# A first product turned round: tokens stationary, 512 weight columns moving

## The chip, the cores and the metric
One NeuronCore of a Trainium2 chip runs the whole program. The metric is device time in microseconds. TensorE multiplies, VectorE and ScalarE do elementwise work and bring results out of PSUM, GpSimd (POOL) does some elementwise work in SBUF, and SyncE (SP) issues the DMAs.

## The reference
Three stages follow one another. `r, k, v, w` have the shape (4, 8, 768, 48); `x` becomes 3072 tokens of 384 values.
```
# attention, per batch and head, over t:
y[t] = r[t] @ (state + (u*k[t]) outer v[t]);  state = w[t]*state + k[t] outer v[t]
# feed-forward, w_in is float64 in memory:
h = x @ w_in            # 3072 x 2048
g = h * cos(h);  x2 = g @ w_out        # 3072 x 384
# soft mixture of experts, 8 experts of 4 slots:
logits = x2 @ phi;  d = softmax over tokens;  slot_input = d.T @ x2
slot_out[e] = relu(slot_input[e] @ w1[e]) @ w2[e]
out = softmax over slots(logits) @ slot_out
```

## The kernel before
The tokens are cut into 24 blocks of 128 (index j) for attention and into 12 groups of 256 (index g) for the feed-forward part. The weights come as float64 and are decoded to float32 by integer steps (raw, abs, mx, d1, d2a, d2b); w_in is then kept as two rounded parts, hi and lo, in four tiles `wu` of 512 columns (whi, wn, wc). x is kept as two parts too (xh, xl), so that one product of the pair needs three matmuls per 128 of the 384 contracted rows: hi by hi, hi by lo, lo by hi.

The first product is b_h (L448 to L464): for a tile (g, i), i from 0 to 7, and each half mm it takes 128 columns of w_in as the stationary block and moves 256 tokens, 9 matmuls a half. A tile is 128 features by 512 (two halves of 256 tokens) in one PSUM bank. Four elementwise steps make g = h cos h of it: turns (ScalarE, L474), rest (VectorE, L478), cos (ScalarE, L482), mul (VectorE, L486). The logits are formed without the second product: p_sb holds w_out @ phi, and l (b_l, L507) multiplies g by it. gT (L494) transposes g on TensorE to tokens by features, gc (L499) copies it from PSUM to SBUF as `gt`, and E (s_e_pe, L603) sums the tokens of `gt` with the softmax weights dt. Between l and E of a group lie sum, lc, max, exp, xt, xr, xd, dT and dc: the logits gathered, the running maximum, the exponentials, and their transpose. es adds a group's E to the running sum. After the last group come si (the sum times w_out, L778), the experts (L797, L837) and the output (L868, L870).

Every step's place is written out by hand in the list HEAD: one string with names such as `h.3.1`, and each engine runs its instructions in the order of the list, SP its DMAs too. Buffers: g has 4, gt 12, the PSUM pools for h, gT, l 2, 1 and 1, and ps_a, shared by attention and late tiles, 3. A step that takes a new buffer waits for the last reader of the old one. "close" gives the decoding buffers back, "att" those of attention and issues the first six loads of expert weights; "we" issues five more, which take the place of wu tiles and of x.

Of the kernel before, what the change touches and what calls it, by code (L numbers as in the profile page):

```python
# [21 lines left out]
def rwkv_moe_kernel(ctx: ExitStack, tc: tile.TileContext, r, k, v, w, u, w_in, w_out, phi, w1, w2, cst, out):  # L22
# [7 lines left out]
    C = 64  # L30
# [6 lines left out]
    NBK = MF // 2  # L37
# [16 lines left out]
    g_p = b_stack.enter_context(tc.tile_pool(name="g", bufs=4, side="right"))  # L54
    gt_p = b_stack.enter_context(tc.tile_pool(name="gt", bufs=12, side="right"))
# [50 lines left out]
    vn_t, rz_t, l_t, ks_t, ksn_t, q_t, bv_t, z_t = ({} for _ in range(8))  # L106
# [243 lines left out]
    def e_abs(x, n, hf=None):  # L350
        if not hf:
# [94 lines left out]
    LAST = (NG - 1, NBK - 1)  # L446

    def b_h(g, i, mm):  # L448
        if mm == 0:
            pool, tag = (ps_a, "a") if NBK * g + i >= ATT else (ps_h, "h")  # L450
            hp = pool.tile([128, 2, G], F32, tag=tag, name=f"h{g}_{i}")
            h_t[g, i] = [hp[:, 0], hp[:, 1], hp]
        elif (g, i) == LAST:
            h_t[g, i][1] = ps_t.tile([128, 2, G], F32, tag="t", name=f"h{g}_{i}b")[:, 0]
        hp = h_t[g, i][mm]
        xh, xl = xh_t[g], xl_t[g]
        m = 2 * i + mm
# [12 lines left out]
    def b_turns(g, i, mm=None):  # L470
        if not mm:
            g_t[g, i] = g_p.tile([128, 2, G], F32, tag="g", name=f"g{g}_{i}")
        gt, hp = bank(g, i, mm)
        nc.scalar.activation(gt.bitcast(I32), hp, AF.Copy, bias=0.25, scale=1.0 / TWO_PI)  # L474

    def b_rest(g, i, mm=None):
        gt, hp = bank(g, i, mm)
        nc.vector.scalar_tensor_tensor(out=gt, in0=gt.bitcast(I32), scalar=-TWO_PI, in1=hp, op0=ALU.mult, op1=ALU.add)  # L478

    def b_cos(g, i, mm=None):  # L480
        gt, _ = bank(g, i, mm)
# [35 lines left out]
    def s_logits(g):  # L517
# [62 lines left out]
    def s_dc(g):  # L582
# [4 lines left out]
        sm[g] = (dt_, *sm[g][0:2])  # L587
# [58 lines left out]
    if True:  # L646
# [54 lines left out]
        step = {"tab": exp_table, "quart": lambda g: s_quarters(g, sm[g][0]), "esl": lambda g, hf: s_e(g, slice(hf * 256, hf * 256 + 256)),  # L701
# [57 lines left out]
        with tc.manual_schedule(engines=ORDERED):  # L759
# [155 lines left out]
raw.o.0 abs.o.1 mx.o.1 U.1 st.1.0 lr.3 d1.o.1 y.0 z.1.1 wf.2 yb.0 xh.0 lz.1 rz.1.0 d2a.o.1 xl.0 whi.0 wn.0.0 st.1.1 wc.0.0 lk.2
kT.2 scan.2 wn.0.1 abs.o.0 rz.1.1 d2b.o.1 mx.o.0 abs.o.2 ks.2 d1.o.0 mx.o.2 d2a.o.0 y.1 bv.1 yb.1 oT.3 oc.3 sr.2 d1.o.2 lr.2
wc.0.1 xh.1 raw.i.1 z.2.0 d2b.o.0 abs.i.1 kN.2 xl.1 oT.2 oT.1 ksn.2 oc.2 oc.1 d2a.o.2 oT.0 oc.0 mx.i.1 lw.4 h.0.2.0 d2b.o.2 oT.5
rT.2 lv.2 d1.i.1 d2a.i.1 raw.i.4 abs.i.4 h.0.2.1 oc.5 sp.2 d2b.i.1 oT.4 oc.4 lw.3 lk.3 lz.2 wT.3 whi.1 wf.3 om.0 L.2 mx.i.4 d1.i.4
# [150 lines left out]
```

## Time and profile before

| | before |
|---|---|
| runs | 542.59, 543.63, 544.12 us |
| median of the runs | 543.63 us |
| span of the profiled execution | 542.5 us |
| TensorE busy | 502.9 us, 93% |
| VectorE busy | 435.2 us, 80% |
| ScalarE busy | 310.7 us, 57% |
| granted TensorE clock, mean | 0.980 |

The span runs from the first to the last instruction of the profiled execution; its own time is that span and the little around it, and it stands 1.1 us below the median of the runs. A matmul's busy time is its latency, some 0.28 us, and matmuls overlap; the pace is read from start to start.

### The profile page before, as it was taken

Reading aid. Unit: us, or ns where it says so; the run is one execution under the profiler, and the core shown is the slowest. Engines: PE = TensorE matmul, PEld = TensorE weight load, DVE = VectorE, ACT = ScalarE, POOL = GpSimd, SP = SyncE. Lnnn points to the kernel's source line nnn. Section 1 sums busy time; section 2 is a strip of 40 time slices with the busy share of each in tenths; the row PEclk is TensorE's granted clock in tenths of the full one; section 3 lists DMA queues with packets and bytes.
Section 4 is the critical chain, followed back from the end, with each engine's and each line's share of the span. In section 5 each row is a group of like instructions: output and inputs, shape, how many; then the busy total and the mean of one; then the engine's idle time right before and its main releaser. Section 6 shows DMA issues by size and latency. Waiting matters only on the chain.

```text
span 542.5 us, 16245 instructions
## 1 busy us (share of the span) xinstructions
PE 502.9 (93%) x6850; PEld 436.4 (80%) x6850; DVE 435.2 (80%) x826; ACT 310.7 (57%) x655; POOL 125.4 (23%) x163
## 2 busy tenths in 40 slices
PE   2769879989999999999999999999999999998994
PEld 1547668879898898999988989989998989894673
DVE  4999998998889879887879788989878877666423
ACT  3356567646747555676555665755657646666421
POOL 4520120254044213221420331352033100000400
PEclk9977998999999999999999999999999999999998
DMA  9994656444332432421440442065031565188958
GB/s 218 258 238 105 176 115 183 125 76 75 74 59 46 76 59 50 79 37 30 76 74 1 75 89 45 17 111 83 16 61 31 229 252 220 29 322 311 403 181 272
DMA packets 146713, 67.52 MB, mean 124 GB/s; under 512 B 127569, under 2 KB 134737, under 8 KB 146641
## 3 DMA queue, kind: packets, MB, share of 16 engines
q1 hardware_dynamic: 146640, 66.49, 48.4%
q8 instruction: 54, 0.88, 0.7%
q14 instruction: 19, 0.15, 0.1%
HBM read 61.75 MB, written 4.72 MB: 123 GB/s over the span
## 4 chain that ended last, share of the span: by engine, by line
PE 67%; DVE 18%; ACT 5%; DMA 4%; issue 2%; SPq 2%; DVEq 0%; ACTq 0%
PE h L462 10%; PE h L464 10%; PE h L463 10%; PE gT L494 6%; PE l L507 4%; PE E L603 3%; PE A L208 3%; PE y L288 3%; PE U L259 2%; DMA vz<-in_v_dram 2%; PE hps L797 2%; DMA rawi<-in_moe_w_in_dram 2%; PE so L837 2%; DVE L L222 2%; DVE pt L164 2%
## 5 line engine op out<-in xcount | busy, mean ns | idle before, releaser
L462 PE MATMUL h<-x,wu 128*128 128x256 f32 x573 | 171.5, 299 | 1.4 <-DVE g L486 1.3
L464 PE MATMUL h<-x,wu 128*128 128x256 f32 x573 | 160.9, 281 | 0.0
L463 PE MATMUL h<-x,wu 128*128 128x256 f32 x573 | 160.8, 281 | 0.0
L462 PEld LDWEIGHTS h<-x,wu 128*128 128x128 f32 x573 | 108.7, 190 | 3.6 <-DVE g L486 1.7
L463 PEld LDWEIGHTS h<-x,wu 128*128 128x128 f32 x573 | 108.8, 190 | 0.2
L464 PEld LDWEIGHTS h<-x,wu 128*128 128x128 f32 x573 | 108.5, 189 | 0.0
L482 ACT ACTIVATE g<-g,half_pi 128x512 f32<-128x512 f32 (+1 forms) x97 | 69.4, 719 | 44.7 <-DVE g L478 43.7
L486 DVE TENSOR_TENSOR g<-g,h 128x512 f32<-128x512 f32 x96 | 64.8, 677 | 26.7 <-ACT g L482 26.1
L474 ACT ACTIVATE g<-h 128x512 int32<-128x512 f32 x96 | 57.1, 596 | 42.0 <-PE h L464 32.6
L478 DVE SCALAR_TENSOR_TENSOR g<-g,h 128x512 f32<-128x512 int32 x96 | 65.0, 678 | 14.9 <-ACT g L474 13.9
L251 POOL TENSOR_TENSOR bv<-vz,bo 64x384 f32<-64x384 f32 x48 | 43.8, 914 | 139.5 <-DVE bo L243 54.6
L499 ACT COPY gt<-gT 128x512 f32<-128x512 f32 x89 | 51.6, 584 | 28.7 <-PE gT L494 28.1
L494 PE MATMUL gT<-cs,g 128*128 128x128 f32 x384 | 58.1, 275 | 0.3 <-ACT gt L499 0.2
L494 PEld LDWEIGHTS gT<-cs,g 128*128 128x128 f32 x384 | 43.7, 140 | 6.0 <-issue 3.7
L169 POOL TENSOR_TENSOR ru<-rn,u_b 128x384 f32<-128x384 f32 x24 | 27.5, 1145 | 57.2 <-issue 19.5
L193 POOL MEMSET L<- 64x512 f32 x32 | 16.6, 520 | 96.0 <-PE y L288 81.5
L156 DVE TENSOR_TENSOR_SCAN qt<-wf,one_b 128x520 f32<-128x520 f32 x24 | 30.6, 1275 | 7.3 <-ACT wf L151 7.3
L222 DVE TENSOR_TENSOR L<-A,cs 64x512 f32<-64x512 f32 x48 | 33.0, 688 | 4.0 <-PE A L208 2.9
L274 ACT COPY rzs<-z 64x192 f32<-64x192 f32 x96 | 33.4, 348 | 3.6 <-DVE z L269 2.6
L187 DVE TENSOR_TENSOR L<-rT,pt 64x512 f32<-64x512 f32 x48 | 32.9, 686 | 1.6 <-PE rT L141 0.6
L164 DVE TENSOR_TENSOR_SCAN pt<-wf,ini_f 128x520 f32<-128x520 f32 x24 | 31.7, 1320 | 0.1
L208 PE MATMUL A<-L,ks 128*64 128x64 f32 (+1 forms) x768 | 27.7, 223 | 3.2 <-DVE ks L199 2.1
(172 smaller groups left out, 837.8 us busy)
## 6 DMA issues: line engine op xcount, KB each, us to landing
we<-in_moe_w_dram SPq DMA_DIRECT2D x16, 1536.0 KB, 10.4
rawi<-in_moe_w_in_dram SPq DMA_DIRECT2D x7, 768.0 KB, 5.5
wn<-in_w_dram SPq DMA_DIRECT2D x24, 192.0 KB, 4.0
kn<-in_k_dram SPq DMA_DIRECT2D x24, 192.0 KB, 4.0
rn<-in_r_dram SPq DMA_DIRECT2D x24, 192.0 KB, 3.8
vz<-in_v_dram SPq DMA_DIRECT2D x48, 96.0 KB, 3.1
rzs<-in_v_dram SPq DMA_DIRECT2D x96, 48.0 KB, 2.8
out_dram<-ob SPq DMA_DIRECT2D x17, 256.0 KB, 3.6
```

Source lines behind the costliest of these rows:

```text
L208: nc.tensor.matmul(ps[64 - 64 * a:128 - 64 * a, s, :], lhsT=ks[k, s, :], rhs=L[k, a, s, :], start=True, stop=True)
L222: nc.vector.tensor_tensor(out=L[h, a], in0=ps[h], in1=mask[h].unsqueeze(1).to_broadcast([64, NS, C]), op=ALU.mult)
L251: nc.gpsimd.tensor_tensor(out=bv[h], in0=vn_t[j][h, :, c, :], in1=bo[h].to_broadcast([64, H, D]), op=ALU.mult)
L462: nc.tensor.matmul(hp, lhsT=wh, rhs=xh[:, c, :], start=(c == 0), stop=False)
L463: nc.tensor.matmul(hp, lhsT=wh, rhs=xl[:, c, :], start=False, stop=False)
L464: nc.tensor.matmul(hp, lhsT=wl, rhs=xh[:, c, :], start=False, stop=(c == KD - 1))
L474: nc.scalar.activation(gt.bitcast(I32), hp, AF.Copy, bias=0.25, scale=1.0 / TWO_PI)
L478: nc.vector.scalar_tensor_tensor(out=gt, in0=gt.bitcast(I32), scalar=-TWO_PI, in1=hp, op0=ALU.mult, op1=ALU.add)
L482: nc.scalar.activation(gt, gt, AF.Sin, bias=half_pi[:, 0:1])
L486: nc.vector.tensor_tensor(out=gt, in0=gt, in1=hp, op=ALU.mult)
L494: nc.tensor.transpose(ps[:, tt, mm, :], gt[:, mm, tt * 128:(tt + 1) * 128], ident)
L499: (nc.vector.tensor_copy if NBK * g + i >= ATT and i in (1, 2, 5) else nc.scalar.copy)(t, pend.pop(("gT", g, i)))
```

## The change
b_h takes a tile of 128 tokens (index t, 24 of them) and 512 columns of w_in (index q, 4 of them). xh and xl of the 128 tokens are the stationary block now, and wu moves: 9 matmuls of 512 columns a tile, the result tokens by features. So g has tokens on the partitions: E reads it directly, with 4 matmuls of 512 columns for each block of tokens, and l reads the transposed copy, with 128 columns, in 96 calls instead of 48. The pools become 13 buffers for g and 3 for gt; the transposed w_out tiles of the start (oc) take theirs from the g pool. All steps stand in a new list of 1929 names instead of 1977; with the halves of h joined, h has 96 entries instead of 192. Some dictionaries go, and some tiles are created by whichever step comes first. The core of the diff follows.

```diff
-    NBK = MF // 2
+    NBK = 4
+    NGB = 13
-    g_p = b_stack.enter_context(tc.tile_pool(name="g", bufs=4, side="right"))
-    gt_p = b_stack.enter_context(tc.tile_pool(name="gt", bufs=12, side="right"))
+    g_p = b_stack.enter_context(tc.tile_pool(name="g", bufs=NGB, side="right"))
+    gt_p = b_stack.enter_context(tc.tile_pool(name="gt", bufs=16 - NGB, side="right"))
...
-    def b_h(g, i, mm):
...
+    def b_h(t, q):
+
+        late = NBK * t + q >= ATT
+        hp = (ps_a if late else ps_h).tile([128, 512], F32, tag="a" if late else "h", name=f"h{t}_{q}")
+        cols = [slice(0, 512)]
+        h_t[t, q] = [hp]
+        if (t, q) == LAST:
+            cols = [slice(0, 256), slice(256, 512)]
+            h_t[t, q] = [hp, ps_t.tile([128, 512], F32, tag="t", name=f"h{t}_{q}b")]
+        o = (t % 2) * TB
+        xh, xl = (x[:, :, o:o + TB] for x in (xh_t[t // 2], xl_t[t // 2]))
+        for half, f in zip(h_t[t, q], cols):
+            for c in range(KD):
+                wh, wl = wu[q][:, 0, c, f], wu[q][:, 1, c, f]
+                nc.tensor.matmul(half[:, f], lhsT=xh[:, c, :], rhs=wh, start=(c == 0), stop=False)
+                nc.tensor.matmul(half[:, f], lhsT=xl[:, c, :], rhs=wh, start=False, stop=False)
+                nc.tensor.matmul(half[:, f], lhsT=xh[:, c, :], rhs=wl, start=False, stop=(c == KD - 1))
...
+    def b_l(t, q):
+
+        g, first = t // 2, t // 2 not in lps_t
+        if first:
             lps_t[g] = ps_l.tile([128, 512], F32, tag="l", name=f"l{g}")
...
+        o, gt = (t % 2) * TB, gt_t.pop((t, q))
+        for m in range(4):
+            nc.tensor.matmul(lps_t[g][32 * m:32 * m + 32, o:o + TB], lhsT=p_sb[:, 4 * q + m, :], rhs=gt[:, m * 128:(m + 1) * 128],
+                             start=first, stop=False, skip_group_check=True)
...
-        for tt in range(2):
+        cols, tiles = (slice(part * 256, part * 256 + 256), (0, 1)) if g == NG - 1 else (slice(0, 512), (part,))
+        for tt in tiles:
             for q in range(4):
-                nc.tensor.matmul(ps[32 * q:32 * q + 32, hf * 256:(hf + 1) * 256], lhsT=dt_[:, tt, :],
-                                 rhs=gt_t[g, 4 * hf + q][:, tt, :], start=(tt == 0), stop=(tt == 1))
...
+                nc.tensor.matmul(ps[32 * q:32 * q + 32, cols], lhsT=dt_[:, tt, :], rhs=g_t[2 * g + tt, q][:, cols], start=(tt == 0), stop=(tt == 1))
...
-                    c, q, qq = (m // 8) * 2 + m % 2, (m % 8) // 2, m % 4
+                    c, q, qq = m % 4, m // 4, m % 4
```

The first and the last lines of the new list:

```
lw.0 lk.0 wT.0 kT.0 wf.0 raw.i.2 z.0.0 misc lr.0 rT.0 lw.1 abs.i.2 raw.i.0.0 lw.2 scan.0 sr.0 lv.0 abs.i.0.0 ru.0 raw.i.0.1
...
wT.10 h.4.3 turns.5.0 wf.10 xr.1 gc.4.0 rT.9 xd.1 turns.4.3 mask.8 gT.4.2 dT.1 rest.5.0 kN.9 xl.7 ltok.1 cos.5.0 U.8 l.4.0
l.4.1 rest.4.3 st.8.0 gc.4.2 dc.1 E.1.0 mul.5.0 cos.4.3 mul.4.3 z.8.1 h.5.2 scan.10 gT.4.3 h.5.1 L.9 rz.8.0 turns.5.2
...
cos.23.2 h.22.3 lc.10 max.10 gT.22.1 mul.23.2 turns.22.3 exp.10 gT.22.0 xt.10 xr.10 h.23.0 xd.10 rest.22.3 dT.10 ltok.10 att
dc.10 h.22.2 cos.22.3 gc.22.0 turns.22.2 E.10.0 mul.22.3 h.23.3 turns.23.0 we.10 cmb.2.5 gc.22.1 rest.22.2 cos.22.2
turns.23.3.1 gT.22.3 rest.23.0 mul.22.2 cos.23.0 rest.23.3.1 mul.23.0 h.23.1 cos.23.3.1 gT.23.0 turns.23.3.0 l.22.0 l.22.1
rest.23.3.0 gc.22.3 mul.23.3.1 gT.22.2 turns.23.1 cos.23.3.0 gc.23.0 we.6 gT.23.2 we.8 rest.23.1 cos.23.1 gc.22.2 l.23.0
gc.23.2 l.22.2 mul.23.1 mul.23.3.0 l.22.3 gT.23.1 gT.23.3 we.7 cmb.2.6 gc.23.3 tab we.9 gc.23.1 l.23.1 l.23.2 l.23.3 sum.11
lc.11 max.11 E.10.1 quart.11 es.10 exp.11 dT.11 dc.11 E.11.0 E.11.1 ltok.11 esl.11.0 esl.11.1
```

## Rows read from the trace of the kernel before

**Rows 1.** The page: engines; a group (busy us, mean ns | idle us); loads of weights.

```profile
PE 502.9 (93%) x6850; PEld 436.4 (80%) x6850; DVE 435.2 (80%) x826; ACT 310.7 (57%) x655; POOL 125.4 (23%) x163
...
L462 PE MATMUL h<-x,wu 128*128 128x256 f32 x573 | 171.5, 299 | 1.4 <-DVE g L486 1.3
...
we<-in_moe_w_dram SPq DMA_DIRECT2D x16, 1536.0 KB, 10.4
```

**Rows 2.** Stretches: start:end length, busy us and instructions by engine, clock, DMA.

```profile
core 0: us, PE busy (x) PEld busy (x) DVE busy (x) ACT busy (x) POOL busy (x), PEclk, DMA share, GB/s
0.00:115.00 115.00, 88.94 (x1025) 71.30 (x1026) 102.85 (x160) 63.70 (x121) 29.67 (x46) 0.93 0.75 175
115.00:484.00 369.00, 365.28 (x5096) 331.42 (x5095) 307.08 (x604) 223.37 (x478) 89.06 (x108) 1.00 0.36 84
484.00:499.00 15.00, 12.99 (x144) 8.60 (x143) 9.91 (x29) 9.50 (x25) 0.82 (x1) 1.00 0.73 262
```

**Rows 3.** The chain that ended last, by line.

```profile
by line: PE h L462 10.0%; PE h L464 9.8%; PE h L463 9.8%; PE gT L494 6.1%; PE l L507 3.6%; PE E L603 3.4%; PE A L208 3.1%; PE y L288 2.9%; PE U L259 2.4%; issue 2.3%; DMA vz<-in_v_dram 2.1%; PE hps L797 2.0%; DMA rawi<-in_moe_w_in_dram 2.0%
```

**Rows 4.** Groups of TensorE by line from 115 to 484 us.

```profile
L462 PE MATMUL h<-x,wu 128*128 128x256 f32 x513 | 153.4, 299 | 0.6 <-DVE g L486 0.6
```

**Rows 5.** TensorE in order: start, us, then line, tiles, count; two halves of h.

```profile
301.65 0.36 PE L462 MATMUL h<-x,wu 128*128 128x256 f32 x1
301.86 0.28 PE L463 MATMUL h<-x,wu 128*128 128x256 f32 x1
...
303.76 0.28 PE L464 MATMUL h<-x,wu 128*128 128x256 f32 x1
```

**Rows 6.** TensorE in order, four halves late: second and 36th matmul.

```profile
480.38 0.28 PE L463 MATMUL h<-x,wu 128*128 128x256 f32 x1
...
484.24 0.28 PE L464 MATMUL h<-x,wu 128*128 128x256 f32 x1
```

**Rows 7.** TensorE in order, the output product of 128 columns.

```profile
532.47 2.45 PE L870 MATMUL o<-sr,cr 96*128 96x128 f32 x20
```

**Rows 8.** TensorE in order, the first product of five experts.

```profile
503.54 6.68 PE L797 MATMUL hps<-we,zs 128*32 128x256 f32 x120
```

**Rows 9.** TensorE in order: l, phi product, and what follows; y, l, gT.

```profile
116.97 0.64 PE L507 MATMUL l<-g,p_sb 128*32 128x256 f32 x8
117.43 1.08 PE L429 MATMUL pt<-wt,phi_sb 128*32 128x128 f32 x24
118.44 0.66 PE L141 MATMUL kT<-cs,kn 128*128 128x128 f32 x4
...
313.28 1.08 PE L288 MATMUL y<-L,rzs 128*32 128x64 f32 x64
314.17 0.61 PE L507 MATMUL l<-g,p_sb 128*32 128x256 f32 x8
314.72 0.66 PE L494 MATMUL gT<-cs,g 128*128 128x128 f32 x4
```

**Rows 10.** TensorE in order: E of a group, and what follows.

```profile
363.40 1.93 PE L603 MATMUL E<-gt,dt 128*32 128x256 f32 x32
365.26 0.65 PE L141 MATMUL rT<-cs,rn 128*128 128x128 f32 x4
```

**Rows 11.** Groups of VectorE and ScalarE from 115 to 484 us.

```profile
L486 DVE TENSOR_TENSOR g<-g,h 128x512 f32<-128x512 f32 x86 | 58.4, 680 | 26.3 <-ACT g L482 25.8
L478 DVE SCALAR_TENSOR_TENSOR g<-g,h 128x512 f32<-128x512 int32 x86 | 58.2, 678 | 14.3 <-ACT g L474 13.3
...
L482 ACT ACTIVATE g<-g,half_pi 128x512 f32<-128x512 f32 x86 | 61.8, 721 | 43.2 <-DVE g L478 42.5
```

**Rows 12.** TensorE in order: last matmul of h, E of group 11.

```profile
487.90 0.28 PE L464 MATMUL h<-x,wu 128*128 128x256 f32 x1
...
496.13 2.15 PE L603 MATMUL E<-gt,dt 128*32 128x256 f32 x32
```

**Rows 13.** SP's issues of expert weights in order of time.

```profile
424.48 47.71 SPq L678 DMA_DIRECT2D we<-in_moe_w_dram  x7
...
488.21 18.56 SPq L682 DMA_DIRECT2D we<-in_moe_w_dram  x7
```

More of the change, by code (lines that the diff above doesn't have):

```diff
@@ L915 @@
[L915 to L918, printed above, removed]
@@ L979 @@
-mul.6.4 dc.5 h.6.7.1 wT.18 kN.17 turns.6.7 E.5.0 l.6.5 rest.6.7 cos.6.7 mul.6.7 wf.18 yb.15 xh.15 xl.15 cmb.1.1 cmb.1.4 h.6.6.0
-gT.6.2 gc.6.2 h.6.6.1 gT.6.5 gc.6.5 turns.6.6 scan.18 cmb.1.2 rest.6.6 cos.6.6 E.5.1 y.16 yb.16 xh.16 h.7.1.0 h.7.1.1 ru.18 zl.18
-turns.7.1 gT.6.4 rT.18 sr.18 sp.18 mul.6.6 l.6.7 ksn.17 U.17 rest.7.1 cos.7.1 xl.16 gc.6.4 L.18 A.17 gT.6.6 gc.6.6 mask.17 st.17.0
-cmb.1.3 es.5 sum.6 mul.7.1 wT.19 h.7.0.0 h.7.0.1 gT.6.7 gc.6.7 lc.6 max.6 rz.17.0 turns.7.0 exp.6 kT.18 ks.18 h.7.2.0 h.7.2.1
@@ L999 @@
-l.8.7 rz.22.1 turns.9.1 rest.9.1 z.23.0 cos.9.1 gT.8.4 sum.8 gc.8.4 lk.23 kT.23 lz.23 h.9.0.0 bo.22 sr.23 h.9.0.1 turns.9.0 lv.23
-lc.8 mul.9.1 h.9.3.0 ks.23 kN.23 h.9.3.1 yb.21 mask.22 ksn.23 U.23 rest.9.0 y.22 cos.9.0 turns.9.3 rz.23.0 mul.9.0 rest.9.3 ru.23
-l.9.1 bv.22 yb.22 gT.9.0 cos.9.3 max.8 exp.8 st.23.0 mul.9.3 bo.23 xh.22 gc.9.0 z.23.1 st.23.1 xt.8 xr.8 xd.8 h.9.2.0 h.9.2.1
-turns.9.2 rT.23 dT.8 h.9.4.0 xl.22 cmb.1.5 zl.23 rest.9.2 sp.23 cos.9.2 gT.9.1 L.23 gc.9.1 h.9.4.1 gT.8.6 h.9.5.0 h.9.5.1 gc.8.6
@@ new lines @@
+mul.3.3 rz.7.0 gT.3.1 L.8 h.4.0 wf.9 lk.9 rest.4.1 cos.4.1 mul.4.1 U.7 turns.4.0 lv.8 bv.7 st.7.0 A.8 lr.10 gc.3.1 rest.4.0 lz.8 gT.3.3 h.4.2 z.7.1
+bo.8 st.7.1 scan.9 cos.4.0 sr.9 sp.9 lw.10 kN.8 gc.3.3 gT.4.1 rz.7.1 l.3.1 lk.10 lv.9 turns.4.2 l.3.2 l.3.3 lw.11 ksn.8 rest.4.2 lr.9 y.7 gc.4.1 zl.9
+mul.4.0 bv.8 es.0 sum.1 yb.7 gT.4.0 cos.4.2 z.8.0 xh.7 lc.1 ru.10 kT.9 h.5.0 max.1 mul.4.2 exp.1 ks.9 xt.1 wT.10 h.4.3 turns.5.0 wf.10 xr.1 gc.4.0
+rT.9 xd.1 turns.4.3 mask.8 gT.4.2 dT.1 rest.5.0 kN.9 xl.7 ltok.1 cos.5.0 U.8 l.4.0 l.4.1 rest.4.3 st.8.0 gc.4.2 dc.1 E.1.0 mul.5.0 cos.4.3 mul.4.3
@@ new lines @@
+cos.7.3 rz.10.0 ks.12 gT.7.1 mul.7.3 turns.7.2 rest.7.2 xl.9 cmb.0.3 cos.7.2 cmb.0.4 kN.12 gc.7.1 ksn.12 lk.13 lw.13 h.8.0 gT.7.0 turns.8.0 rT.12
+mul.7.2 y.10 gc.7.0 cmb.0.2 bo.11 z.11.1 l.7.0 l.7.1 rest.8.0 cos.8.0 l.6.3 gT.7.2 sp.12 gc.7.2 yb.10 h.8.1 mul.8.0 lr.13 gT.7.3 turns.8.1 st.11.1
+L.12 lr.14 xh.10 ru.13 z.12.0 h.8.2 l.7.2 rest.8.1 gc.7.3 zl.12 turns.8.2 rest.8.2 cos.8.1 bv.11 bo.13 l.7.3 U.12 sum.3 mul.8.1 lv.13 A.12 rz.11.1
+cos.8.2 bv.12 st.12.0 lc.3 max.3 gT.8.1 exp.3 gc.8.1 h.8.3 turns.8.3 z.12.1 st.12.1 xt.3 xr.3 mul.8.2 lk.14 xd.3 wT.13 rz.12.1 wf.13 gT.8.0 rest.8.3
@@ new lines @@
+mul.17.3 rT.22 gT.17.3 lz.22 h.18.1 rest.17.2 cos.17.2 wf.23 kN.22 gc.17.3 yb.20 xh.20 mul.17.2 gT.17.0 z.22.0 turns.18.1 h.18.0 ksn.22 gc.17.0
+gT.17.2 zl.22 l.17.0 gc.17.2 rest.18.1 scan.23 L.22 xl.20 cos.18.1 turns.18.0 l.17.1 rz.22.0 y.21 l.17.2 rest.18.0 mul.18.1 l.17.3 U.22 sum.8 A.22
+yb.21 h.18.3 mask.22 lc.8 st.22.0 z.22.1 xh.21 kT.23 gT.18.1 st.22.1 cos.18.0 h.19.2 max.8 xl.21 z.23.0 exp.8 mul.18.0 h.19.1 turns.18.3 ks.23
+rest.18.3 gc.18.1 cos.18.3 turns.19.2 gT.18.0 zl.23 xt.8 xr.8 xd.8 kN.23 rest.19.2 gc.18.0 dT.8 bo.22 cos.19.2 mul.18.3 h.19.0 rz.22.1 ltok.8 h.18.2
@@ L1019 @@
+gT.23.2 we.8 rest.23.1 cos.23.1 gc.22.2 l.23.0 gc.23.2 l.22.2 mul.23.1 mul.23.3.0 l.22.3 gT.23.1 gT.23.3 we.7 cmb.2.6 gc.23.3 tab we.9 gc.23.1 l.23.1
+l.23.2 l.23.3 sum.11 lc.11 max.11 E.10.1 quart.11 es.10 exp.11 dT.11 dc.11 E.11.0 E.11.1 ltok.11 esl.11.0 esl.11.1
 """
```

294 lines of the change are left out of this document (126 added, 168 removed).

## The prediction

> **What bounds the kernel now.** I read first the busy times of the engines, then stretches of the span, then the order of TensorE's instructions inside the long stretch. TensorE is busy for 502.9 of 542.5 us [rows 1]; that is an average, so the stretches decide. From 0 to 115 us VectorE is busy for 102.9 us and TensorE for 88.9: decoding of the weights and the first attention blocks set the pace, and TensorE has gaps. From 115 to 484 us TensorE is busy for 365.3 of 369 us, with a granted clock of 1.00, VectorE for 307.1 (83%). From 484 to 499 us a chain through several engines ends the token groups; TensorE is busy for 13 of 15 us [rows 2]. In the chain that ended last the three lines of the first product stand first, with 29.6% of the span [rows 3]. So time taken from TensorE between 115 and 484 us is time taken from the kernel; time taken from it before 115 us is not. That stretch holds 513 [rows 4] of the 573 matmuls of L462 that the trace lists [rows 1], nine tenths.
>
> **The first product.** Before: 96 tiles of 18 matmuls with 256 columns moving, 1728 in all. In the middle the second matmul of a run starts at 301.86 and the eighteenth at 303.76 us: 0.119 us from start to start; the first takes 0.21, so entering a run costs 0.09 [rows 5]. Late, without attention between, 34 intervals take 3.86 us, 0.1135 each [rows 6]. At 2.4 GHz (the clock column's 1.00) 256 columns need 0.107 us, so what is the other 0.012? Two rows answer. The output product at L870 moves only 128 columns, half as many, over a stationary block of the same 128 columns: 20 in 2.45 us, less the 0.28 that one lasts [rows 5], over 19 intervals, is 0.114 each [rows 7]. Halving the columns gained nothing: loading a block of 128 columns costs about 0.114 us whatever moves, and 256 columns just fail to hide it. And the expert product at L797, in float32, four strips of the array side by side, each instruction equal to 512 column cycles: 120 instructions in 6.68 us, 6.68/120x4 = 0.223 per 512 cycles at most, since the run's entry and the end of its last instruction are in it; the columns alone are 0.213 [rows 8].
>
> After: 96 tiles of 9 matmuls with 512 columns, 864. The load of 0.114 lies inside 0.213 of columns. Bounds: 0.213 (columns alone) and 0.238 (twice 0.119). Nearest is the L797 row, so I take 0.220, its 0.223 less a little for the ends. The first product stands in 117 separate runs on TensorE in the list before, and in 92 in the new one. Before: 1728x0.119 + 117x0.09 = 216.2 us. After: 864x0.220 + 92x0.09 = 198.4. Saved 17.8, nine tenths of it in the stretch that counts: **-16.0** (bounds: -21.2 and -2.1).
>
> The Trainium skill speaks against this, in "TensorE: Matmul & The Clock Gate", section "Back-to-back issue gap": an isolated stream is spaced by the columns at 2.4 GHz plus 2.5 ns. By that the product takes 1728x0.1092 = 188.7 us before and 864x0.2158 = 186.5 after, an estimate from that page: 2 us saved, and the kernel slower once the next terms are paid. The rows of before do not follow it (0.119, not 0.109).
>
> **Logits (l).** Before 48 calls of four matmuls with 256 columns; after 96 calls with 128 columns. The column time is the same. One call before takes 0.46 us (116.97 to 117.43) or 0.55 (314.17 to 314.72), of which the columns are 0.427, so 0.505x48 = 24.2 us. For 128 columns the phi product at L429 has exactly this form: 12 in 1.01 us, 0.337 per four; 96x0.337 = 32.3, so +8.1 at most. At the other end the y product, with 64 columns and 32-column blocks, runs 64 instructions in 0.89 us, 0.0139 each where columns alone need 0.0133, so short ones need not be slow; then only the 17 more runs (55 against 38) cost, about 0.12 each (0.55-0.427): +2.0 [rows 9]. I take +4.5 between them; nine tenths of it: **+4.0**.
>
> **E.** It reads g, in 8 matmuls of 512 columns a group instead of 16 of 256. A group takes 1.86 us where columns need 1.71 [rows 10]; half the starts, **-0.5** (0 to -1.5). The transposes, the copies gc, and the four elementwise steps keep number and shape.
>
> **Pools.** A g tile now lives until E of its group. Thirteen buffers are eight of the group and five ahead, so turns of the sixth tile of the next group waits for E. In the new list E.1.0 stands after turns.5.0 and before turns.5.2, so the list respects it. Behind a late turns on ScalarE stand the copies gc and ksn, which TensorE waits for. Before, 12 gt and 4 g buffers gave four and four ahead, so this is tighter but not new. gt needs three buffers because l follows gc at once. The dropped dictionaries and the conditions on tile creation issue nothing. The order of the si product changes only which blocks of et it reads.
>
> **End of the groups.** Before, the last h matmul starts at 487.90 and E of group 11 at 496.13 us, 8.2 us [rows 12]. The last l now needs the last transpose (0.66 to its end [rows 9]) and its copy (ScalarE takes 0.72 for cos on the same shape [rows 11]) before sum, lc, max, exp and dT; E no longer waits for those copies. Part of it is covered by the l of other tiles: +1. In the new list only gT.22.1, gT.22.0 and h.23.0 (2.8 us) stand between lc.10 and dT.10. Of the 8.2 us four elementwise steps of 0.7 are 2.8, which leaves 5.4 for l, sum, lc, max, exp, dT and its copy; I put two thirds of that, 3.6, on max, exp, xt, xr and xd as an estimate, so TensorE waits for another +1. Together **+2** (0 to +4).
>
> **Waits.** The work of VectorE does not shrink. In the middle it holds 307.1 us; in a stretch 13 us shorter its share rises from 83 to 86%. Its idle time there is mostly that before rest and mul, 14.3 and 26.3 us, waiting for ScalarE, which waits 43.2 us before cos for VectorE [rows 11]: two engines that pass a tile back and forth, with two PSUM buffers for h as before. Some of it will come to TensorE: **+2** (0 to +8). The head has the same decoding and the same attention steps in another order; SP's loads stand in nearly the same sequence (lk.0 moves ahead of raw.i.2, lv.0 ahead of raw.i.0.1). I take nothing for it, and +-3 for the range.
>
> **Expert loads.** Attention ends later: after xl.23 12 tiles of h are left, against 16.5. SP issued the first of w1 at 424.48 us and the last seven of all loads from 488.21 [rows 13]. Four tiles, some 13 us, go from the time for the six first loads; TensorE still has about 40 us of work before E.11 is done (12 tiles at 2.07 for h, 0.8 for gT and l, and E). A load has 1536 KB [rows 1]; at the 262 GB/s that the end of the groups moved with 0.73 of the queue's time [rows 2] a full queue moves 359 GB/s, 4.4 us a load, 31 us for the six and we.10. They fit: 0.
>
> **Sum.** -16.0+4.0-0.5+2+2 = -8.5. The profiled execution spans 542.5 us; the runs have a median of 543.6, 1.1 more, which I carry over: 534.0+1.1 = **535**.
>
> **Rivals.**
> *The 0.012 belongs to the columns, not to the load* (reads of SBUF that other engines slow down). For it: late, with attention gone, the same matmul takes 0.1135 instead of 0.119. Against it: the L870 row. Then 512 columns take 0.238, h gives 2.1, and l and the end still cost: -2.1+4.0-0.5+2+1 = +4.4, **548**. It decides from a spacing of 0.231, where the saving of h (8.3 us, nine tenths of it 7.5) equals the other terms. The gap rule of the Trainium skill gives the same outcome by another road. Chance 0.14.
> *VectorE and ScalarE are the bound already.* If the back-and-forth of a tile cannot go faster, the middle stays 369 us and only the end changes: **544.5**. For it: 83% and the waits of rows 11. Against it: TensorE's 365 of 369, with VectorE idle for 62 us. Chance 0.12, mostly no change.
> *The expert loads come late.* If one load of 4.4 us is still under way when L797 wants it, L797 waits for it: **539**. Chance 0.08.
> *Columns alone* (0.213) and no new waits: -21.2+1.8-1+1 = -19 us, **524**. Chance 0.08.
> My forecast, 529 to 541: chance 0.58.
>
> **Numbers.** A difference of 0.3% (1.6 us, about the spread 542.59 to 544.12) is what can be told from none. Faster by more: 0.58+0.08+0.08 and little of the second rival, 0.75; within: 0.10; slower: 0.15. The range takes in most of the fast case and the slow one's near side: 526 to 547.
>
> **What would show it.** In the profile after: h with 512 columns spaced 0.216 to 0.225; l taking 0.29 to 0.33 a call; TensorE still busy for more than 96% of the middle, VectorE's share at 86%; the time from the last h to E.11 at 9 to 10 us; no idle time before L797. The forecast is wrong if the spacing is above 0.231, if ScalarE's turns is released by E often, or if the gaps of TensorE before 115 us grow.

## The result and the profile after

| | before | after |
|---|---|---|
| median of the runs | 543.88 us (542.59 to 544.86, 4 runs) | 535.55 us (534.27 to 537.09, 4 runs) |
| span of the profiled execution | 542.5 us | 533.8 us |

The profiled execution of the kernel after took 535.62 us. The ratio is 0.9847, with an interval from 0.982 to 0.9873: 8.3 us faster. The forecast was 535, in a range from 526 to 547. The total is right; the terms behind it are not, as the rows show.

The page of the kernel after, answering to [rows 1]: engines with busy time, share and count; the chain that ended last by engine; two groups (busy us, mean ns | idle us); the loads of expert weights.

```profile
PE 495.2 (93%) x6203; PEld 391.3 (73%) x6203; DVE 433.0 (81%) x826; ACT 308.3 (58%) x655; POOL 128.5 (24%) x163
...
PE 69%; DVE 21%; ACT 5%; issue 2%; DMA 1%; SPq 0%; ACTq 0%; DVEq 0%
...
L461 PE MATMUL h<-wu,x 128*128 128x512 f32 x288 | 121.0, 420 | 1.3 <-DVE g L488 1.3
...
we<-in_moe_w_dram SPq DMA_DIRECT2D x16, 1536.0 KB, 10.6
```

Stretches of the span of the kernel after, to be held against [rows 2].

```profile
0.00:115.00 115.00, 89.44 (x1056) 68.76 (x1058) 107.15 (x165) 66.13 (x129) 29.89 (x47) 0.93 0.78 173
115.00:475.00 360.00, 357.71 (x4422) 289.48 (x4417) 301.51 (x604) 219.80 (x473) 91.93 (x107) 1.00 0.37 84
475.00:490.00 15.00, 12.13 (x142) 7.56 (x142) 9.34 (x26) 8.43 (x22) 0.82 (x1) 1.00 0.81 302
```

The long stretch became nine us shorter, and TensorE is as full in it as before (357.7 of 360, 99%). In the head TensorE is as busy as before (89.4 us against 88.9), while VectorE does 4.3 us more of its work there, so VectorE's share of the middle is 84%, not 86%.

TensorE's instructions in order, kernel after: start, us, line, tiles, count. First come a tile of h in the middle and the runs behind it, then the second and last matmul of a tile late, without attention, then the last matmul of h and the end of the groups (in brackets the idle time and its releaser).

```profile
304.68 0.48 PE L461 MATMUL h<-wu,x 128*128 128x512 f32 x1
305.00 0.40 PE L462 MATMUL h<-wu,x 128*128 128x512 f32 x1
...
306.62 0.40 PE L463 MATMUL h<-wu,x 128*128 128x512 f32 x1
306.95 0.64 PE L510 MATMUL l<-gt,p_sb 128*32 128x128 f32 x16
307.42 1.10 PE L287 MATMUL y<-L,rzs 128*32 128x64 f32 x64
308.34 1.04 PE L606 MATMUL E<-g,dt 128*32 128x512 f32 x8
309.31 0.66 PE L495 MATMUL gT<-cs,g 128*128 128x128 f32 x4
...
469.23 0.39 PE L462 MATMUL h<-wu,x 128*128 128x512 f32 x1
...
470.84 0.39 PE L463 MATMUL h<-wu,x 128*128 128x512 f32 x1
...
477.18 0.40 PE L463 MATMUL h<-wu,x 128*128 128x512 f32 x1
...
482.06 0.86 PE L510 MATMUL l<-gt,p_sb 128*32 128x128 f32 x24 [0.35 <-DVE gt L501]
483.47 0.70 PE L523 MATMUL lc<-lg,cs 128*128 128x256 f32 x2 [0.55 <-DVE lg L517]
486.04 0.33 PE L580 MATMUL dT<-cs,dl 128*128 128x128 f32 x1 [0.87 <-ACT dl L552]
486.88 1.93 PE L606 MATMUL E<-g,dt 128*32 128x256 f32 x32 [0.51 <-ACT dt L587]
```

From 305.00 to 306.62 lie 7 intervals: 0.231 each. From 469.23 to 470.84 again 7: 0.230. The first product is spaced 0.2305, not 0.220, and it is not faster when attention is gone. The 16 instructions of l are two calls (four matmuls a call, each recorded as two instructions), and they take 0.47 us (306.95 to 307.42); by the median over the stretch it is 0.24 to 0.28 a call, depending on how many calls stand in a row, where 0.29 to 0.33 was expected. From the last h to the last E it is 9.7 us (477.18 to 486.88), against 8.2 in [rows 12].

Where TensorE's time went, from 115 us to the last matmul of h. Each run of one kind counts from its start to the start of the next run, so waits inside count too. The table is worked out from the order of TensorE's instructions; y is its product with L alone, om the product of w_out and phi, and oT the transposes of w_out for it.

| us | h | gT | l | y | A | E | U | lc | om, oT | last h at |
|---|---|---|---|---|---|---|---|---|---|---|
| before | 199.4 | 35.6 | 23.4 | 19.5 | 19.1 | 18.1 | 13.9 | 4.0 | 1.8 | 487.9 |
| after | 190.0 | 37.1 | 23.6 | 17.3 | 18.5 | 18.8 | 13.7 | 4.9 | 0 | 477.2 |
| difference | -9.4 | +1.5 | +0.2 | -2.1 | -0.6 | +0.7 | -0.1 | +0.8 | -1.8 | -10.7 |

About 87 of the 96 tiles of h lie in this stretch in both kernels. Of 10.7 us, h gave 9.4. The steps y, A, U, om and oT, whose work the change doesn't touch, gave another 4.6: some of them stand ahead of 115 us in the new list (om and oT all, and one block's y), and the rest are entered with less delay. gT, E and lc took 3.0 back, but 0.9 of that is one more half of E that now lies in the stretch (21 against 20). Likewise 83 of the 96 calls of l lie in it, where the 44 of 48 before correspond to 88. Behind the last h the end of the groups lost 1.5 and what follows it 0.6: -10.7+1.5+0.6 = -8.6, the difference of the spans up to rounding.

### The profile page after: what moved, and what is told of

The parts are those of the page before. It is cut to its first block, busy times and chain, and to the rows that moved or that the text cites. A ratio compares the mean times of both kernels' runs of the same rounds, so it can differ in the third digit from the quotient of the medians.

```text
span 533.8 us, 14954 instructions
## 1 busy us (share of the span) xinstructions
PE 495.2 (93%) x6203; PEld 391.3 (73%) x6203; DVE 433.0 (81%) x826; ACT 308.3 (58%) x655; POOL 128.5 (24%) x163
## 4 chain that ended last, share of the span: by engine, by line
PE 69%; DVE 21%; ACT 5%; issue 2%; DMA 1%; SPq 0%; ACTq 0%; DVEq 0%
PE h L461 10%; PE h L463 9%; PE h L462 9%; PE gT L495 7%; PE l L510 4%; PE A L207 4%; PE y L287 3%; PE E L606 3%; PE U L258 3%; DVE g L480 2%; DVE L L221 2%; PE hps L797 2%; PE so L837 2%; PE wl L403 2%; DVE g L488 2%
## 5 line engine op out<-in xcount | busy, mean ns | idle before, releaser
L461 PE MATMUL h<-wu,x 128*128 128x512 f32 x288 | 121.0, 420 | 1.3 <-DVE g L488 1.3
L463 PE MATMUL h<-wu,x 128*128 128x512 f32 x288 | 113.2, 393 | 0.0
L462 PE MATMUL h<-wu,x 128*128 128x512 f32 x288 | 112.7, 391 | 0.0
L476 ACT ACTIVATE g<-h 128x512 int32<-128x512 f32 (+1 forms) x96 | 56.8, 595 | 49.7 <-PE h L463 40.9
L480 DVE SCALAR_TENSOR_TENSOR g<-g,h 128x512 f32<-128x512 int32 (+1 forms) x96 | 64.6, 677 | 24.9 <-ACT g L476 24.1
L488 DVE TENSOR_TENSOR g<-g,h 128x512 f32<-128x512 f32 x96 | 64.2, 673 | 14.0 <-ACT g L484 13.3
L250 POOL TENSOR_TENSOR bv<-vz,bo 64x384 f32<-64x384 f32 x48 | 45.4, 947 | 89.2 <-DVE bo L242 38.6
L461 PEld LDWEIGHTS h<-wu,x 128*128 128x128 f32 x288 | 54.2, 188 | 15.3 <-DVE g L488 4.2
L463 PEld LDWEIGHTS h<-wu,x 128*128 128x128 f32 x288 | 54.1, 188 | 12.0
L462 PEld LDWEIGHTS h<-wu,x 128*128 128x128 f32 x288 | 54.4, 189 | 8.5
L495 PEld LDWEIGHTS gT<-cs,g 128*128 128x128 f32 x384 | 45.2, 141 | 9.9 <-issue 2.9
L510 PE MATMUL l<-gt,p_sb 128*32 128x128 f32 x768 | 31.8, 276 | 0.3 <-DVE gt L501 0.3
```

Of the source, the lines that this page charges most:

```text
L250: nc.gpsimd.tensor_tensor(out=bv[h], in0=vz[j % 2][h, :, c, :], in1=bo[h].to_broadcast([64, H, D]), op=ALU.mult)
L461: nc.tensor.matmul(half[:, f], lhsT=xh[:, c, :], rhs=wh, start=(c == 0), stop=False)
L462: nc.tensor.matmul(half[:, f], lhsT=xl[:, c, :], rhs=wh, start=False, stop=False)
L463: nc.tensor.matmul(half[:, f], lhsT=xh[:, c, :], rhs=wl, start=False, stop=(c == KD - 1))
L495: nc.tensor.transpose(ps[:, m * 128:(m + 1) * 128], gt[:, m * 128:(m + 1) * 128], ident)
L510: nc.tensor.matmul(lps_t[g][32 * m:32 * m + 32, o:o + TB], lhsT=p_sb[:, 4 * q + m, :], rhs=gt[:, m * 128:(m + 1) * 128], start=first, stop ...
```

## The experiments

The theory to be tested was the prediction's: the stationary load takes 0.114 us, so only its unhidden 0.012 is saved by wider matmuls, and nine tenths of what TensorE saves comes to the end. Each run stands against the kernel before on the same chip (544.36 us for the first four, 544.79 for the last four). Differences to the kernel after are taken from the medians; taken from the ratios they would be up to 1.1 us other (10 us of e2_pass would be 9.6, 17.7 of e6_both 18.8), which changes none of the readings.

### e1_halves: the new kernel, each tile in two runs of 256 columns

```diff
+        if (t, q) != LAST:
+            cols = [slice(0, 256), slice(256, 512)]
-        for half, f in zip(h_t[t, q], cols):
+        for half, f in zip(h_t[t, q] if (t, q) == LAST else [hp, hp], cols):
```

> The changed kernel, but each tile of the first product is made in two runs of 256 columns of w_in (18 matmuls, tokens still stationary) in the same list and the same buffers. The trace of the changed kernel has both forms: 512 columns are spaced 0.2305 us, the 256-column halves of its last tile 0.1175. Theory 1 (the width gives the gain, because the load of a stationary block hides behind 512 columns): 18x0.1175 against 9x0.2305 is 0.04 us more a tile, +3.9 us on TensorE, nine tenths of it in the end: 539 us. Theory 2 (as the prediction had it, 0.119 a matmul of 256 columns whatever stands): 0.067 a tile, +5.8 us: 541. Rival (the gain came from the new list and the cheaper l, the width does nothing): within 1 us of 535.5.

Measured: 540.9 us (540.13 to 541.01), ratio to before 0.9942 (0.9923 to 0.996). A run of h, in order:

```profile
300.90 0.28 PE L464 MATMUL h<-wu,x 128*128 128x256 f32 x1
...
304.97 0.28 PE L465 MATMUL h<-wu,x 128*128 128x256 f32 x1
```

34 intervals: 0.1197 each. So the exchange of operands alone does not change the pace of a matmul of 256 columns (0.119 in [rows 5]; where x lies in a tile of its own, as told under h below, the two differ by up to 0.004). The width is worth 540.9-535.6 = 5.3 us of the 8.3, and h in the stretch of the table is 195.1 us here, 5.1 more than after; no other column of the table differs from after by more than 0.4. The other 3 us came from the new list and the other steps, not from the width. The list shortened h too: at the same width h takes 199.4 before and 195.1 here, 4.3 less, because it stands in 83 runs instead of 102 in the stretch (19x0.09 = 1.7), and with shorter pauses behind the runs.

### e2_pass: the new kernel without one pass of h

The low part of x is left out in the last third of the contraction: 8 matmuls a tile instead of 9, so 96x0.2305 = 22.1 us less for TensorE, and nothing less for any other engine.

```diff
-                nc.tensor.matmul(half[:, f], lhsT=xl[:, c, :], rhs=wh, start=False, stop=False)
+                if c < KD - 1:
+                    nc.tensor.matmul(half[:, f], lhsT=xl[:, c, :], rhs=wh, start=False, stop=False)
```

> The changed kernel without one of the nine matmuls of a tile (the low part of x in the last third of the contraction is left out). TensorE loses 0.2305x96 = 22 us of work, the list is the same. If TensorE alone sets the middle, nine tenths of it come back: 515.5 us. Rival: VectorE, busy 84% of the middle, and the hand-over between VectorE and ScalarE already limit it; then half of it or less comes back, 525 us or more.

Measured: 525.62 us, ratio 0.967 (0.9644 to 0.9695): 10 us below after, 0.45 of what was taken. First a stretch of the middle:

```profile
115.00:465.00 350.00, 341.43 (x4324) 272.38 (x4322) 300.63 (x604) 218.58 (x471) 92.64 (x107) 1.00 0.38 86
```

then a wait of TensorE's loads of stationary blocks (us, times, longest):

```profile
PEld h L461 <- DVE g L489: 9.0, 17, 1.0
```

and the chain by engine:

```profile
PE 43%; DVE 39%; ACT 10%; issue 4%; DMA 3%; POOL 0%; SPq 0%; ACTq 0%; DVEq 0%; POOLq 0%
```

In the kernel after, the same stretch and then the same wait read:

```profile
115.00:465.00 350.00, 347.85 (x4363) 282.19 (x4359) 294.38 (x584) 214.20 (x458) 91.93 (x107) 1.00 0.37 82
```

```profile
PEld h L461 <- DVE g L488: 4.2, 10, 0.8
```

TensorE's idle time in 350 us goes from 2.2 to 8.6 us; h waits 9.0 us for VectorE to release its PSUM buffer instead of 4.2; and VectorE's part of the chain goes from 21% to 39%. Counted as in the table, h fell by 18.1 us, while gT and l, which wait for what VectorE and ScalarE bring, took 2.8 and 2.0 more. So of a cut of this size on TensorE alone less than half comes back, with the list as it stood; no run remade the list for the shorter product.

### e3_rest: the new kernel with half of rest

rest works on 256 of 512 columns (the other half of g is left unfinished): VectorE has 25 us less to do, TensorE the same.

```diff
+        if hf is None:
+            gt, hp = gt[:, 0:256], hp[:, 0:256]
```

> The changed kernel with the step rest done on half of the columns only (the other half of g keeps the integers of turns). VectorE loses about 0.26x95 = 25 us, 7% of its share of the middle, and a link of the chain turns, rest, cos, mul becomes shorter. If TensorE sets the middle: 1 to 3 us less, from the head and the end of the groups, 533 to 535. Rival (VectorE or the hand-over limits the middle): 5 to 12 us less, 524 to 531.

Measured: 532.24 us, ratio 0.9777 (0.9752 to 0.9803): 3.3 us below after. Its chain by engine:

```profile
PE 79%; DVE 13%; ACT 3%; DMA 3%; issue 2%; SPq 0%; ACTq 0%; DVEq 0%
```

VectorE's 21% falls to 13% and TensorE's 69% rises to 79%, but the time hardly falls. VectorE was not the bound either.

### e4_burst: matmuls by themselves

Behind the last outputs TensorE runs alone: 18 matmuls of 512 columns, 36 of 256, 36 of 128, each over three blocks of 128 columns in turn, then 18 of 512 over blocks of 32 and of 64 columns. The output is unchanged.

```diff
+            wide_ = cr[:, 0, 0:4, :].rearrange("p b t -> p (b t)")
+            for i, (m, n, k) in enumerate(((128, 512, 18), (128, 256, 36), (128, 128, 36), (32, 512, 18), (64, 512, 18))):
+                ps = pb(f"burst{i}")
+                for j in range(k):
+                    nc.tensor.matmul(ps[0:m, 0:n], lhsT=cr[:, 1 + j % 3, 0, 0:m], rhs=wide_[:, 0:n], start=(j == 0), stop=(j == k - 1))
```

> The changed kernel with five bursts on TensorE behind its last output product, operands of the output product (96 rows), no other compute engine at work: 18 matmuls of 512 columns over a stationary block of 128 columns, 36 of 256, 36 of 128, and 18 of 512 over blocks of 32 and of 64 columns. Load theory: 128 and 256 columns both at about 0.114 us, 512 at 0.213 to 0.220. Rival (a cost for each matmul beside its columns): 512 stays at 0.228 to 0.231 here too, and 256 near 0.119. If the excess over 0.213 comes from the change of the stationary block, it shrinks with blocks of 64 and 32 columns; if it comes from other engines in SBUF, it is gone in all of the bursts.

One execution: 550.31 us. The five bursts as groups (stationary block, then columns):

```profile
L912 PE MATMUL burst<-cr 96*128 96x256 f32 x36 | 4.5, 283 | 0.0
L912 PE MATMUL burst<-cr 96*32 96x512 f32 x18 | 4.3, 393 | 0.0
L912 PE MATMUL burst<-cr 96*128 96x512 f32 x18 | 4.3, 393 | 0.0
L912 PE MATMUL burst<-cr 96*64 96x512 f32 x18 | 4.3, 392 | 0.0
L912 PE MATMUL burst<-cr 96*128 96x128 f32 x36 | 4.1, 273 | 0.0
```

Three stretches inside them, laid out as in [rows 2]; every other engine is idle. The first two lie in the burst of 256 columns, while the outputs are still being stored (DMA share 0.98) and after that (0.03); the third lies in the burst of 128 and the start of the one of 512 over blocks of 32, without DMA:

```profile
531.10:533.00 1.90, 1.90 (x18) 1.90 (x17) 0.00 (x0) 0.00 (x0) 0.00 (x0) 1.00 0.98 274
533.20:535.30 2.10, 2.10 (x21) 2.10 (x19) 0.00 (x0) 0.00 (x0) 0.00 (x0) 1.00 0.03 8
536.00:540.00 4.00, 4.00 (x35) 3.62 (x34) 0.00 (x0) 0.00 (x0) 0.00 (x0) 1.00 0.00 0
```

The busy time less one latency, over the intervals: 128 columns (4.1-0.273)/35 = 0.109; 256 columns (4.5-0.283)/35 = 0.1205; 512 columns (4.3-0.393)/17 = 0.230, over blocks of 32, 64 and 128 alike. Starts read one by one in the timeline give 0.111, 0.120, and 0.2275, 0.231 and 0.230. At 2.4 GHz the columns alone are 0.053, 0.107 and 0.213. So 512 columns cost 0.014 to 0.018 more than the columns alone and 256 cost 0.013: the excess comes with each matmul, hardly grows with the columns, and is there over a block of 32 columns as over one of 128. By the forecast's theory a load of 0.11 would have vanished behind 0.213 of columns. Engines that disturb are absent (but for the first microsecond of the first burst, when the last copies of the output end), and the stores change nothing: the 256 columns keep to 0.120 with them and without. Both readings of the 0.012 fall, the forecast's (the load) and its first rival's (the columns under contention). Only at 128 columns does the spacing show another limit, 0.11. One reading was not tested: every matmul here changes its stationary block, so a fixed cost of that change, whatever the block's size, can't be told from a cost of the matmul itself.

### e5_oldorder: the new steps in the old kernel's order

The old list is carried over: tile (g, i) becomes token block 2g+i%2 and quarter i//2, h stands where its second half stood, l behind the next gT. Steps are put off until their inputs and buffers are there.

```diff
-lw.0 lk.0 wT.0 kT.0 wf.0 raw.i.2 z.0.0 misc lr.0 rT.0 lw.1 abs.i.2 raw.i.0.0 lw.2 scan.0 sr.0 lv.0 abs.i.0.0 ru.0 raw.i.0.1
...
(the list of the kernel after, replaced by the old one with its names mapped)
```

> The changed kernel with its steps in the order of the list before: tile (g, i) becomes tile (2g + i mod 2, i div 2), h stands where the second half of the old tile stood, l comes behind the next transpose, and a step that would need a buffer or an input not yet there moves back to the first place where it can stand. The two-run experiment left 3.4 us of gain that the width does not explain. Theory (the new list brings those): without it the kernel is 3 to 6 us slower than the changed one, 539 to 542. Rival (the list brings nothing, the 3.4 us are the cheaper terms l and U): 535 to 537. If the old order fits the new tiles badly (the E of a group late, turns waiting for a g buffer), it is slower than before, over 545.

Measured: 665.38 us, ratio 1.2212 (1.2172 to 1.2252). Two stretches:

```profile
300.00:400.00 100.00, 88.41 (x1012) 66.46 (x1011) 72.33 (x143) 51.59 (x111) 18.95 (x23) 1.00 0.28 49
...
500.00:600.00 100.00, 73.42 (x551) 51.55 (x549) 45.17 (x103) 39.55 (x83) 0.00 (x0) 0.85 0.40 150
```

Three waits (us, times, longest):

```profile
DVE mx L531 <- PE lc L523: 36.5, 11, 7.3
...
ACT g L476 <- PE E L606: 23.2, 11, 6.2
...
PEld h L461 <- DVE g L488: 17.1, 7, 4.6
```

No engine is full in either stretch, and the waits go back and forth between them: the softmax waits 36.5 us for lc, eleven times, turns waits 23.2 us for E, and h's loads wait for VectorE. In the mapped list sum, lc, max and exp often follow one another directly (in group 7 they hold four places in a row, where the new list spreads them over 21); that this is what makes the waits is likely but not shown. What the new order is worth with the old steps can't be told from this run: the mapping itself costs some 120 us, far more than what was to be measured.

### e6_both: the cuts of e2_pass and e3_rest together

The edit is both diffs above; the output lacks what both leave out.

> The changed kernel with both cuts of the earlier runs: one of the nine matmuls of a tile left out and rest on half of the columns. Alone they gave 10 us (of 22 taken from TensorE) and 3.3 us (of 25 taken from VectorE). Theory (the two engines hold each other up through the two PSUM buffers of h, so a cut on one shows up as waiting for the other): together clearly more than 13 us, 18 to 22: 514 to 518 us. Rival (the cuts are independent and something else, such as the head, keeps the rest): 13 to 14 us, 522.

Measured: 517.92 us, ratio 0.9502 (0.9471 to 0.9534): 17.7 us below after, where the two cuts alone gave 10.0+3.3 = 13.3. Its chain by engine:

```profile
PE 58%; DVE 24%; ACT 8%; DMA 6%; issue 3%; SPq 0%; ACTq 0%; DVEq 0%
```

Each cut is worth 4.4 us more once the other is made. That is how two engines behave that take turns in holding each other up: neither is the bound alone. Nor is VectorE's load the whole of it: with its cut made first, the cut of h returns 17.7-3.3 = 14.4 of 22.1 us, two thirds and not nine tenths. What keeps the rest was not traced.

### e7_before_pass: the cut of e2_pass in the kernel before

Was the poor return new, or was it there before? The same low part is left out of the old kernel: 192x0.119 = 22.8 us less for TensorE.

```diff
-            nc.tensor.matmul(hp, lhsT=wh, rhs=xl[:, c, :], start=False, stop=False)
+            if c < KD - 1:
+                nc.tensor.matmul(hp, lhsT=wh, rhs=xl[:, c, :], start=False, stop=False)
```

> The kernel before without the same part: the low part of x in the last third of the contraction, one of nine matmuls of a half, 192x0.119 = 23 us of TensorE's work. Theory (before, TensorE set the middle, and only the new balance with VectorE makes the changed kernel give back less): 18 to 20 us less, 524 to 526. Rival (half came back before, too; the nine tenths of the prediction were too high from the start): 10 to 12 us less, 532 to 534.

Measured: 535.66 us, ratio 0.9833 (0.9804 to 0.9861): 9.1 us back, 0.40 of the cut. Its chain by engine:

```profile
PE 51%; DVE 31%; ACT 10%; issue 3%; DMA 3%; SPq 0%; DVEq 0%; ACTq 0%
```

The page of the kernel before has there:

```profile
PE 67%; DVE 18%; ACT 5%; DMA 4%; issue 2%; SPq 2%; DVEq 0%; ACTq 0%
```

So the old kernel returned no more than the new one. The nine tenths of the prediction were too much for a large cut from the start.

### e8_mask_pool: some of VectorE's work given to GpSimd

For 8 of the 24 token blocks the mask product (two instructions of 0.689 us on VectorE) goes by a copy on ScalarE and a product on GpSimd, by steps (mc and mp) that the kernel defines but that its own list doesn't use.

```diff
-rT.9 xd.1 turns.4.3 mask.8 gT.4.2 dT.1 rest.5.0 kN.9 xl.7 ltok.1 cos.5.0 U.8 l.4.0 l.4.1 rest.4.3 st.8.0 gc.4.2 dc.1 E.1.0 mul.5.0 cos.4.3 mul.4.3
+rT.9 xd.1 turns.4.3 mc.8 mp.8 gT.4.2 dT.1 rest.5.0 kN.9 xl.7 ltok.1 cos.5.0 U.8 l.4.0 l.4.1 rest.4.3 st.8.0 gc.4.2 dc.1 E.1.0 mul.5.0 cos.4.3 mul.4.3
...
(the same for mask.10, 12, 14, 16, 18, 20 and 22)
```

> The changed kernel with the mask step of every second block from 8 on taken from VectorE: ScalarE copies the PSUM tile, GpSimd multiplies by the mask. VectorE loses 8 times 1.37 us, 11 us in all, ScalarE gains as much, GpSimd gains 8 times 2.5 us. By the rest experiment (3.3 us for 25) VectorE's load is worth 1 to 1.5 us: 534 to 535. Rival (the longer way of A to y and ScalarE's extra work cost more than that): 536 to 540.

Measured: 539.87 us (539.03 to 540.93), ratio 0.9913 (0.9883 to 0.9944), 4 us above after. The middle, and then the group of the product on GpSimd:

```profile
115.00:475.00 360.00, 353.87 (x4391) 286.37 (x4390) 292.13 (x580) 224.98 (x481) 114.72 (x123) 1.00 0.36 80
```

```profile
L233 POOL TENSOR_TENSOR L<-L,cs 64x512 f32<-64x512 f32 x16 | 21.1, 1319 | 74.9 <-ACT L L228 59.9 <-PE U L258 14.5
```

VectorE has 9 us less in the middle (292.1 against 301.5), yet TensorE has 3.8 less as well in the same 360 us. The product takes 1.319 us instead of 0.689, and a copy comes ahead of it. So this way of taking work from VectorE costs more than it gives. Which wait costs it stays open: the trace lists no engine as released by GpSimd's product, and what TensorE gives up is spread over several steps (counted as in the table, 0.9 us on h, 1.4 on the transposes of y, 1.1 on those of r).

## Why the prediction came out right, and where its steps did not

**h: mis-sized.** The step that failed is "the 0.012 is the load's unhidden part", with "I take 0.220". Measured is 0.2305, against 0.119 before. By the prediction's own formula that is 1728x0.119 - 864x0.2305 + 25x0.09 = 8.7, nine tenths of it 7.8, where it had 16.0. The table counts 9.4, in two parts: 5.1 for the width (e1_halves against after) and 4.3 for the list (before against e1_halves), of which the prediction had only the fewer runs, 25x0.09. So the width, the heart of the forecast, is worth about a third of what it was to give. What stands in place of the load: a cost that comes with each matmul, 0.013 to 0.018 in e4_burst, which hardly depends on its width; twice as wide a matmul pays it half as often. What it is inside the engine stays open. The row that misled was L870 [rows 7]: 0.114 at 128 columns is a limit of its own at that width, and that it lies close to 0.119 says nothing of the cause. L797 [rows 8] was a bound from other matmuls, in another mode, and not the nearest row after all.

The forecast also read [rows 6] wrongly: 256 columns came every 0.1135 us there, and it took this for an effect of attention being gone, a sign for its first rival. The pace goes with the place of x instead. x of every third group (2, 5, 8 and 11) lies in a tile of its own, that of the others in one shared tile (L307 of the kernel before), and [rows 6] are from group 11. A half of group 6 has 0.119 [rows 5]; a half of group 2, second to eighteenth matmul, with attention running:

```profile
177.40 0.28 PE L463 MATMUL h<-x,wu 128*128 128x256 f32 x1
...
179.21 0.28 PE L464 MATMUL h<-x,wu 128*128 128x256 f32 x1
```

That is 1.81 us over 16 intervals, 0.113 each. Over all halves of the kernel before, the median interval lies between 0.113 and 0.118 in these four groups (in 45 of 64 halves at 0.113 or 0.114) and between 0.117 and 0.120 in the other eight. Group 10, whose matmuls run after attention as those of group 11 do, stays at 0.118 to 0.120. So this row speaks neither for contention nor against a cost of each matmul, but that cost is not one number: 0.007 to 0.013 at 256 columns, by the place of x. Why the place matters is not shown.

The Trainium skill's rule, in "TensorE: Matmul & The Clock Gate", section "Back-to-back issue gap", has the form that e4_burst shows, columns at 2.4 GHz plus a constant for each matmul. Its constant of 2.5 ns is not what the runs show: 13 ns at 256 columns and 14 to 18 at 512 in e4_burst, and 7 ns at 256 in the groups of [rows 6]. With it the wider matmuls would have gained 2 us, by the prediction's estimate; they gained 5.

**l: sized at +4.0, measured +0.2 in the stretch.** The table has 23.4 before and 23.6 after, but five calls more lie outside the stretch than before. Over the whole run, counted the same way, l takes 25.7 us before and 27.8 after, +2.1: a call has a median of 0.24 to 0.28 us, about half of the 0.50 to 0.54 before, and there are 55 runs of it instead of 38. That is the lower end of the forecast (+2.0, the entries of 17 more runs). The columns were taken to cost something between phi (0.337 for four matmuls) and y (0.0139 an instruction); y's end was right, and phi, the same shape, was the wrong likeness.

**E, end of groups, expert loads.** E was to give 0.5. The table has 0.7 more, but for 21 halves instead of 20; a half took 0.90 us before and 0.89 after, 0.3 less over the 24 halves of the run. The end of the groups was to cost +2: the last h to E.11 grew by 1.5, and TensorE waits 0.3 us ahead of dT.10. L797 starts with no wait for a load, as its row shows: the run has no idle time before it and takes 6.68 us, as in [rows 8]. SP issues the first of w1 some 5 us and the last some 10 us earlier than in [rows 13]; its queue in order of time, and the expert product on TensorE:

```profile
419.12 19.15 SPq L678 DMA_DIRECT2D we<-in_moe_w_dram  x6
...
478.03 20.01 SPq L682 DMA_DIRECT2D we<-in_moe_w_dram  x6
```

```profile
494.81 6.68 PE L797 MATMUL hps<-we,zs 128*32 128x256 f32 x120
```

So the third rival didn't come.

**What was not in the sum.** The new list took 4.6 us from y, A, U, om and oT in the stretch that counts, and 2 to 3 us of pauses behind the runs of h; the prediction had no term for either. e1_halves bears it out: 3 us of the gain are there without the wider matmuls. Which places in the list gave it was not settled; e5_oldorder was meant to show it and showed only that the old places don't fit.

**"Time taken from TensorE is time taken from the kernel."** For 20 us this does not hold: 0.45 of it came back after (e2_pass), 0.40 before (e7_before_pass). The busy share (99%) hides it, since VectorE at 84% and ScalarE at 61% of the middle hand tiles on with two PSUM buffers, and in e2_pass the faster TensorE waits for them (h's wait for VectorE goes from 4.2 to 9.0 us). The second rival is thus half right: TensorE isn't the bound alone, nor is VectorE (3.3 of 25 us in e3_rest), and the two cuts together return more than their sum (e6_both). For the width itself the return was large: 5.1 us less of h in the stretch, 5.3 less at the end. That a small cut fits under the waits where a large one doesn't is argued from these two, not shown by a row of sizes.

**g's buffers.** The ScalarE row for it: turns was released by E, which the forecast named as a danger.

```profile
ACT g L476 <- PE E L606: 8.2, 7, 2.9
```

Seven times, 8.2 us in all. What it costs in the end was not measured; other splits of the sixteen buffers, or more of them, were not tried.

**The rivals.** The first (548) needed more than 0.231 by the forecast's own terms, and the spacing of 0.2305 came within a hair of it; that the kernel is faster all the same is owed to l, which cost 0.2 in the stretch instead of 4, and to the list. Columns alone (524) falls with 0.2305. The sum that was measured is -9.4 for h, +0.2 for l, -4.6 for the steps that were moved, +3.0 for gT, E and lc, +0.1 for the rest of the stretch, +2.1 behind it: -8.6. The forecast had -16.0 for h, +4.0 for l, 0 for the order, -0.5 for E, and +2 each for the end and the waits: -8.5. The total was right by luck: h, too large by 6.6, was balanced by 3.8 on l and 4.6 on the order, less 1.2 on E.

## What to carry to other kernels

Before costing a wider matmul, read its spacing at two widths on an undisturbed TensorE: a cost of each matmul and a load that isn't hidden look the same at one width, and by the prediction's formula they give 8 or 16 us here. A stretch with TensorE 99% busy still returned only 0.40 to 0.45 of a 22 us cut, where an engine at 83 to 84% was next in the same hand-over; ask what the second engine does with the time before counting a cut as gained. And where a change brings a new order, the unchanged steps belong in the sum too: they gave 4.6 us here.

## What the hardware showed that was not expected

With no other compute engine at work, matmuls of 512 columns came every 0.2275 to 0.231 us, over stationary blocks of 32, 64 and 128 columns alike, and those of 256 every 0.120, with and without DMA; the excess over the columns, 0.013 to 0.018, did not halve with the columns. At 128 columns the spacing was 0.11, twice the columns' time. In the kernel before, the same matmul of 256 columns came every 0.113 to 0.118 us or every 0.117 to 0.120, by the tile in which its moving operand lies, whether attention ran or not. Four matmuls of 128 columns over 32-column blocks side by side took 0.24 to 0.28 us, about half of what the same four with 256 columns took, though phi's, of the same shape, took 0.337 [rows 9].
